# One buffer for a group's first-layer weights, 512-column matmuls for the leftover tile, and a shifted order, in a fused attention and expert kernel

## The chip, the cores and the metric

The kernel runs as one program on one core of a Trainium2 chip. The metric is device time in microseconds of one execution; lower is better. The engines are TensorE (PE), VectorE (DVE), ScalarE (ACT), GpSimd (POOL) and SyncE (SP), which issues the transfers. Each engine works through its own queue of instructions in program order and waits on semaphores for the others.

## The reference, cut to what matters

```python
# q, k, v: (2, 8, 576, 64); D = 512, E = 4, F = 1024, d_ff = 2048, N = 1152 tokens
x = windowed_causal_attention(q, k, v)            # window 128, linear bias by head
x = x.transpose(0, 2, 1, 3).reshape(1152, 512)
p = domain_probs / (domain_probs.sum(-1, keepdims=True) + 1e-09)
out = 0
for e in range(4):
    out += p[:, e:e + 1] * (np.maximum(x @ w1[e], 0.0) @ w2[e])
h = out @ w_in                                    # w_in, w_out are float64
return ((h * np.cos(h)) @ w_out).astype(np.float32)
```

## The kernel before

**Groups.** The two expert stages are cut into 12 groups of 512 hidden columns: groups 0 to 7 are the four experts' halves (Relu), groups 8 to 11 the last stage (h cos h). A group has a first layer (`pair`, twice, for its halves j = 0 and 1 of 256 columns) and a second layer (`layer2`, nine token tiles of 128 tokens). Every fp32 product is made of three passes over a high and a low part (`PASSES`: hi*hi, hi*lo, lo*hi).

**Tokens.** Tiles 1 to 8 (2 x 512 tokens) go through the first layer by seven block products instead of eight (`pair`, `product`), with 512 columns per matmul. Tile 0, the leftover of 128 tokens, goes through the first layer apart (`left(g)`, L732): its transposed tokens `x0` are the stationary operand and the weights `w1t` move, 256 columns at a time, 12 matmuls for each half j, both into one PSUM bank. Then ACT (L751) takes the Relu into the tile `lt` (groups 8 to 11: a cosine chain), and `turn_rows` (L768 to L771) transposes `lt` on PE, so that tile 0's hidden values are ready for the next group's second layer. `left(g + 1)` runs inside group g's second layer, in two steps called "La" and "Lb" (one half j each); "X" is `turn_rows`.

**Weights.** Raw weights come by DMA into two buffers (`rawp`), and a generator of jobs (`weights`, L207) splits them: ACT copies the high part (L201), POOL subtracts the low part (L178). "raw" is the half itself, "sums" its four block sums (POOL adds into `sm`, then the same split), "second" half of the second layer's weights. A first-layer half takes one of two `w1t` buffers. `order_of` sets the order of a group's jobs, `wq` that of their loads.

**Conversions.** The last stage's weights arrive as float64. `convert` turns them into float32 on the side, 32 pieces: ACT L288, DVE L290 and L294, DVE L298, ACT L300, DVE L303, then a store by SP. L300 may only start when L294 of the same piece is done, and sits in ACT's queue among everything else. They run during groups 0 to 5.

**Order.** `steps(g)` writes the order of PE's work by hand: for each entry of `order` it yields a step, how many stages of the cosine chains to advance, how many jobs to record (`njobs`) and how many conversion yields (`ncv`). `run` records, for each entry, first the PE work of the step, then the jobs, then the conversion yields, and last the rest of the step (for "Lb" that is L751, for a tile the accumulation on DVE, L886). So the place of an entry sets what stands ahead of its last part on ACT and DVE. In groups 1 to 6 the order before is

```python
order = (0, "La", 5, 6, 1, 7, "Lb", 2, 8, 3, "X", 4)
njobs = [1] * 8
ncv = {0: 2, "La": 3, 5: 3, 6: 3, 1: 3, 7: 3, "Lb": 2, 2: 2, 8: 2}
```

where an integer is a token tile of the second layer. In groups 8 to 10 "a5" is the first half of tile 5's matmuls, put ahead while ACT, DVE and POOL finish the cosine of the last products.

Of the kernel before, what the change touches and what calls it, by code (L numbers as in the profile page):

```python
# [11 lines left out]
F32R = mybir.dt.float32r  # L12
# [19 lines left out]
ND = DM // 128  # L32
# [10 lines left out]
PASSES = ((0, 0), (0, 1), (1, 0))  # L43
# [6 lines left out]


@with_exitstack
def tile_kernel(ctx, tc, qT, kT, v, probs, w1, w2, w_in, w_out, out):
    nc = tc.nc
    pool = lambda name, **kw: ctx.enter_context(tc.tile_pool(name=name, **kw))

# [2 lines left out]
    xp = pool("xp", bufs=1)  # L59
    zp = pool("zp", bufs=1)  # L60
    hp = pool("hp", bufs=1)
    w1p = pool("w1p", bufs=2)
    w2p = pool("w2p", bufs=W2S)
    accp = pool("accp", bufs=1)
    rawp = pool("rawp", bufs=RAWS)
# [108 lines left out]
    wi32 = dram.tile([DM, F2], F32, name="wi32")  # L174
    wo32 = dram.tile([F2, DM], F32, name="wo32")

    def sub(eng, out, a, b):
        eng.tensor_tensor(out=out, in0=a, in1=b, op=ALU.subtract)  # L178

    def rows(g):  # L180
        return (g // 2, slice((g % 2) * G, (g % 2 + 1) * G)) if g < NG1 else (None, slice((g - NG1) * G, (g - NG1 + 1) * G))

    raw_t, w_t = {}, {}

    def raw_load(kind, g, j):
        e, fs = rows(g)
        if kind == 1:
            t = rawp.tile([128, ND, 256], F32, name="raw", tag="raw")
            src = (wi32 if e is None else w1[e])[:, fs][:, j * 256 : (j + 1) * 256]
        else:  # L190
            t = rawp.tile([128, 2, DM], F32, name="raw", tag="raw")
            src = (wo32 if e is None else w2[e])[fs, :][j * 256 : (j + 1) * 256, :]
        nc.sync.dma_start(out=t, in_=src.rearrange("(m p) f -> p m f", p=128))
        raw_t[kind, g, j] = t

    def first_part(out, src):

        if mm is None:
            nc.gpsimd.tensor_copy(out, src)
        else:  # L200
            nc.scalar.activation(out=out, in_=src, func=AF.Copy)  # L201

    def weights():


        def two_parts(eng, hi, lo, src):
            n = src.shape[1] // 2  # L207
            for p in range(2):
                s = slice(p * n, (p + 1) * n)
                first_part(hi[:, s], src[:, s])  # L210
                sub(eng, lo[:, s], src[:, s], hi[:, s].bitcast(F32))
                yield

        raws = {}

        def first(g, j):
            raw = raws[j] = raw_t.pop((1, g, j))
            w = w_t[1, g, j] = w1p.tile([128, 2, 2, 1024], F32R, name="w1t", tag="w1t")
            yield from two_parts(nc.gpsimd, w[:, 0, 0], w[:, 1, 0], raw.rearrange("p m f -> p (m f)"))

        def first_sums(g, j):

            raw, w = raws[j], w_t[1, g, j]
            a11, a12 = raw[:, 0:2, 0:128], raw[:, 2:4, 0:128]
            a21, a22 = raw[:, 0:2, 128:256], raw[:, 2:4, 128:256]
            sm = ssp.tile([128, 4, 2, 128], F32, name="sm", tag="sm")
            nc.gpsimd.tensor_tensor(out=sm[:, 0], in0=a21, in1=a22, op=ALU.add)
            sub(nc.gpsimd, sm[:, 1], sm[:, 0], a11)
            yield
            sub(nc.gpsimd, sm[:, 2], a11, a21)  # L230
            sub(nc.gpsimd, sm[:, 3], a12, sm[:, 1])
            yield
            loads_ahead()
            yield from two_parts(nc.gpsimd, w[:, 0, 1], w[:, 1, 1], sm.rearrange("p s m f -> p (s m f)"))

        def second(g, j):
            raw = raw_t.pop((2, g, j))
            w = w_t[2, g, j] = w2p.tile([128, 2, 2, DM], F32R, name="w2t", tag="w2t")
            for f in range(2):
                first_part(w[:, 0, f], raw[:, f])  # L240
                sub(nc.gpsimd, w[:, 1, f], raw[:, f], w[:, 0, f].bitcast(F32))
                if f:
                    loads_ahead()
                yield

        for g in range(NG1 + NG2):
            for todo, j in order_of(g):
                yield from {"raw": first, "sums": first_sums, "second": second}[todo](g, j)

    def order_of(g):  # L250

        if g == 0 or g > NG1:
            return [("raw", 0), ("raw", 1), ("sums", 0), ("sums", 1), ("second", 0), ("second", 1)]
        return [("raw", 0), ("sums", 0), ("second", 0), ("raw", 1), ("sums", 1), ("second", 1)]

    wq = [
        (2 if todo == "second" else 1, g, j)
# [5 lines left out]
    def loads_ahead():  # L263

        if nload[0] < len(wq):
            raw_load(*wq[nload[0]])
            nload[0] += 1
# [64 lines left out]
    x0 = xp.tile([128, 2, ND, 128], F32R, name="x0")  # L332
# [355 lines left out]
    def cosine_rows(ps, out):  # L688

        for _ in cosine(ps, out):  # L690
            yield False

    def chain(c, ch):
        next(ch)
        chains.append((c, ch))
# [35 lines left out]
    def sums():  # L731
        return bank().tile([128, 512], F32, name="o_ps", tag="o_ps")  # L732
# [3 lines left out]
    def left(g):  # L736

        ps = sums()
        for j in range(2):
            for d in range(ND):  # L740
                for a, bb in PASSES:
                    nc.tensor.matmul(  # L742
                        ps[:, j * 256 : (j + 1) * 256], x0[:, bb, d, :],
                        w_t[1, g, j][:, a, 0, d * 256 : (d + 1) * 256],
                        start=(d == 0 and (a, bb) == PASSES[0]),
                        stop=(d == ND - 1 and (a, bb) == PASSES[-1]),
                    )
            yield
        r = rows_t[g] = lp.tile([128, 512], F32, name="lt", tag="lt")
        if g < NG1:  # L750
            nc.scalar.activation(out=r, in_=ps, func=AF.Relu)  # L751
        else:
            chain(0, cosine_rows(ps, r))
# [257 lines left out]
    def steps(g):  # L1011
# [6 lines left out]
        ps = [early.pop(j, None) or pair(g, j, early_kind) for j in range(2)]  # L1018
# [24 lines left out]
        if turn:  # L1043
            order = (0, 1, "f0", 5, "f1", 2, "f5", 6, "f2", 3, "f6", 4, "f3", 7, "f4", 8, "f7")
            njobs = [2, 2, 0, 2, 0, 2]
        elif moe:
            order = (0, "La", 5, 6, 1, 7, "Lb", 2, 8, 3, "X", 4)
            njobs = [1] * 8
            if g == 0:
                order = (0, "La", 5, 6, 1, 7, 2, "Lb", 8, 3, "X", 4)  # L1050
                njobs[0] = 2
                ncv = {5: 1, 6: 2, 1: 3, 7: 3, 2: 3, "Lb": 2, 8: 2}
        elif last:
            order, njobs = ("a5", "a6", "a7", "a8", "a1", 5, 6, 7, 8, 1, 2, 3, 4), []
        else:
            order = ("a5", "a6", "a7", "a8", "a1", "La", 5, 6, 7, "Lb", 8, 1, 2, "X", 3, 4)
            njobs = [0, 0, 0, 0, 0, 1, 1, 1, 1, 1, 1, 1, 1, 1, 1, 2]
        for k, o in enumerate(order):
            m = njobs.pop(0) if njobs else 0
            if isinstance(o, int):  # L1060
# [99 lines left out]
```

## Time and profile before

| | us |
|---|---|
| median of 3 runs | 646.12 (646.05 to 647.6) |
| the profiled execution | 647.3 |
| its span, first to last instruction | 645.5 |
| PE busy | 632.0 (98%) |
| DVE busy | 444.3 (69%) |
| POOL busy | 347.1 (54%) |
| ACT busy | 326.4 (51%) |
| granted TensorE clock, mean | 0.995 of full speed |

The profiled execution's own time is 1.8 us over its span and 1.2 us over the median. "Busy" counts the time in which an engine runs an instruction; matmuls overlap, so a line of the timeline that says 2.88 us for twelve matmuls can be followed by the next line 2.72 us after its start. What a stretch of matmuls takes is therefore read from start to start. In a timeline the bracket behind a row is the idle time of the engine ahead of it and what ended it.

### The profile page before, as it was taken

What the parts mean: (1) busy time and instruction counts of PE and PEld (TensorE: products, weight loads), DVE (VectorE), ACT (ScalarE), POOL (GpSimd) and SP (SyncE); (2) the same over time, 40 slices, a digit from 0 to 9 for tenths busy, and PEclk for the clock granted to TensorE, in tenths of its full rate; (3) what the DMA queues carried; (4) which work ended last, traced back from release to release, by engine and by line L of the source; (5) the groups of instructions that cost most, each with busy time, mean ns of one, the idle gap of its engine ahead of it and who ended that gap; (6) DMA issues with size and microseconds to landing.
All of it is one profiled execution on the core that took longest, in us unless ns stands there. A gap on an engine that the chain in (4) does not pass through costs nothing.

```text
span 645.5 us, 9428 instructions
## 1 busy us (share of the span) xinstructions
PE 632.0 (98%) x3456; PEld 520.6 (81%) x3456; DVE 444.3 (69%) x774; ACT 326.4 (51%) x690; POOL 347.1 (54%) x332
## 2 busy tenths in 40 slices
PE   8999699999999999999999999999999999999998
PEld 6777588888888888888888888888878888888876
DVE  6878658879879878779789543556873574664653
ACT  6998624444444353443443331455883583673650
POOL 1776439264275275185265390493469369379350
PEclk9999899999999999999999999999999999999999
DMA  9541214525517417427144120130001201201003
GB/s 255 140 147 52 98 32 147 156 89 179 164 56 223 146 45 255 125 80 231 65 155 140 32 80 20 34 98 1 26 7 63 69 2 66 65 1 65 17 2 130
DMA packets 39422, 60.66 MB, mean 94 GB/s; under 512 B 4688, under 2 KB 21840, under 8 KB 39376
## 3 DMA queue, kind: packets, MB, share of 16 engines
q1 hardware_dynamic: 38288, 59.67, 29.1%
q8 instruction: 27, 0.44, 0.3%
q10 hardware_dynamic: 1088, 0.39, 0.2%
q14 instruction: 19, 0.16, 0.1%
HBM read 49.30 MB, written 10.75 MB: 93 GB/s over the span
## 4 chain that ended last, share of the span: by engine, by line
PE 87%; ACT 5%; DVE 5%; issue 1%; DMA 1%; ACTq 0%; POOLq 0%; POOL 0%; DVEq 0%
PE o_ps L865 44%; PE o_ps L712 32%; PE o_ps L742 4%; PE x_ps L570 2%; PE s_ps L471 1%; PE t_ps L538 1%; ACT p L488 1%; DVE p L482 1%; DMA k<-kT 1%; ACT xs L342 1%; ACT u L665 1%; PE l_ps L768 1%; DVE tx L178 1%; ACT r L666 1%; PE f_ps L919 1%
## 5 line engine op out<-in xcount | busy, mean ns | idle before, releaser
L865 PE MATMUL o_ps<-w2t,hpair 128*128 128x512 f32 x1140 | 268.5, 392 | 0.6 <-POOL hpair L178 0.6
L865 PEld LDWEIGHTS o_ps<-w2t,hpair 128*128 128x128 f32 x1140 | 211.3, 188 | 44.0 <-POOL hpair L178 1.4
L712 PE MATMUL o_ps<-xs,w1t 128*128 128x512 f32 x720 | 170.3, 392 | 0.6 <-ACT rs L517 0.6
L712 PEld LDWEIGHTS o_ps<-xs,w1t 128*128 128x128 f32 x720 | 135.6, 189 | 29.2 <-ACT rs L517 0.7
L178 POOL TENSOR_TENSOR w1t<-raw,w1t 128x512 fp32r<-128x512 f32 x48 | 64.7, 1363 | 86.1 <-ACT w1t L201 85.8
L178 POOL TENSOR_TENSOR w2t<-raw,w2t 128x512 fp32r<-128x512 f32 x48 | 63.3, 1340 | 64.4 <-ACT w2t L201 64.3
L178 POOL TENSOR_TENSOR w1t<-sm,w1t 128x512 fp32r<-128x512 f32 x48 | 64.1, 1349 | 37.4 <-ACT w1t L201 34.3
L712 PE MATMUL o_ps<-xz,w1t 128*128 128x512 f32 x288 | 70.8, 392 | 0.9 <-DVE c L779 0.8
L178 POOL TENSOR_TENSOR hpair<-u,hpair 128x512 fp32r<-128x512 f32 x32 | 41.7, 1318 | 45.9 <-ACT hpair L685 45.9
L712 PEld LDWEIGHTS o_ps<-xz,w1t 128*128 128x128 f32 x288 | 53.6, 188 | 13.7 <-DVE c L779 2.5
L300 ACT ACTIVATE cr<-cr 128x512 f32<-128x512 f32 x32 | 21.8, 681 | 78.3 <-DVE cv L294 78.3
L886 DVE SCALAR_TENSOR_TENSOR accpair<-o_ps,pr,accpair 128x512 f32<-128x512 f32 x56 | 41.2, 745 | 28.0 <-PE o_ps L865 28.0
L702 DVE SCALAR_TENSOR_TENSOR hpair<-o_ps,hpair 128x512 fp32r<-128x512 f32 x47 | 32.4, 689 | 21.5 <-ACT hpair L701 21.5
L701 ACT ACTIVATE hpair<-o_ps 128x512 fp32r<-128x512 f32 x47 | 28.2, 599 | 36.0 <-DVE o_ps L779 36.0
L201 ACT ACTIVATE w1t<-sm 128x512 fp32r<-128x512 f32 x44 | 27.4, 625 | 30.4 <-POOL sm L178 30.4
L865 PE MATMUL o_ps<-w2t,h 128*128 128x512 f32 x144 | 36.5, 402 | 4.7 <-ACT xz L342 4.6
L742 PEld LDWEIGHTS o_ps<-w1t,x 128*128 128x128 f32 x288 | 37.5, 191 | 2.1 <-issue 0.3
L669 DVE SCALAR_TENSOR_TENSOR u<-r,u 128x512 f32<-128x512 f32 x36 | 30.0, 833 | 13.3 <-ACT r L666 13.2
L742 PE MATMUL o_ps<-w1t,x 128*128 128x256 f32 x288 | 38.4, 283 | 0.0
L701 ACT ACTIVATE hpair<-c 128x512 fp32r<-128x512 f32 x17 | 10.7, 632 | 51.8 <-DVE c L779 50.2
L865 PEld LDWEIGHTS o_ps<-w2t,h 128*128 128x128 f32 x144 | 27.6, 193 | 11.6 <-ACT xz L342 5.0
L892 DVE TENSOR_TENSOR accpair<-o_ps,accpair 128x512 f32<-128x512 f32 x23 | 15.7, 689 | 30.5 <-PE o_ps L865 30.5
(131 smaller groups left out, 891.6 us busy)
## 6 DMA issues: line engine op xcount, KB each, us to landing
raw<-w SPq DMA_DIRECT2D x32, 512.0 KB, 3.7
cr<-w_in SPq DMA_DIRECT2D x16, 512.0 KB, 4.5
cr<-w_out SPq DMA_DIRECT2D x16, 512.0 KB, 3.9
wi<-cv SPq DMA_DIRECT2D x16, 256.0 KB, 3.5
wo<-cv SPq DMA_DIRECT2D x16, 256.0 KB, 2.2
raw<-wi SPq DMA_DIRECT2D x8, 512.0 KB, 3.4
raw<-wo SPq DMA_DIRECT2D x8, 512.0 KB, 3.6
qt<-qT SPq DMA_DIRECT2D x8, 256.0 KB, 3.8
```

Of the source, the lines that this page charges most:

```text
L178: eng.tensor_tensor(out=out, in0=a, in1=b, op=ALU.subtract)
L201: nc.scalar.activation(out=out, in_=src, func=AF.Copy)
L300: nc.scalar.activation(out=fl(hw), in_=fl(hw), func=AF.Abs)
L570: nc.tensor.matmul(xt[64 * hh : 64 * hh + 64, 2 * g + m, :], v_t[b, j][:ln, 64 * h : 64 * h + 64], pT[:ln, 2 * m + hh, bi, :], start=(bi = ...
L669: nc.vector.scalar_tensor_tensor(out=u, in0=r, scalar=MAGIC, in1=u, op0=ALU.subtract, op1=ALU.subtract)
L701: nc.scalar.activation(out=hi, in_=src, func=AF.Relu)
L702: nc.vector.scalar_tensor_tensor(out=lo, in0=src, scalar=0.0, in1=hi.bitcast(F32), op0=ALU.max, op1=ALU.subtract)
L712: nc.tensor.matmul(ps, w(a, k, m), operand_of_x(bb, b)[:, m], start=(start and m == 0 and (a, bb) == PASSES[0]), stop=(stop and m == 1 and ...
L742: nc.tensor.matmul(ps[:, j * 256 : (j + 1) * 256], x0[:, bb, d, :], w_t[1, g, j][:, a, 0, d * 256 : (d + 1) * 256], start=(d == 0 and (a, ...
L865: nc.tensor.matmul(ps, hidden(a, f, t), w_t[2, g, f // 2][:, bb, f % 2, :], start=(f == 0 and (a, bb) == PASSES[0]), stop=(f == NFG - 1 an ...
L886: nc.vector.scalar_tensor_tensor(out=o, in0=ps, scalar=s, in1=o, op0=ALU.mult, op1=ALU.add)
L892: nc.vector.tensor_tensor(out=o, in0=ps, in1=o, op=ALU.add)
```

## The change

One tile `w1` holds both halves of a group's first-layer weights; each job writes its half of it. `left` moves 512 columns, 256 of each half, in one matmul, and its two steps are now the first and the last two blocks of the contraction instead of the two halves. Since both halves are then needed at "La", a group's jobs are recorded in another order (raw and sums of both halves ahead of "second"), "La" and "Lb" come later in the second layer, and groups 8 to 10 put one more tile ("a2") ahead.

```diff
--- before.py
+++ after.py
@@ -50,7 +50,7 @@
 
 
 @with_exitstack
-def tile_kernel(ctx, tc, qT, kT, v, probs, w1, w2, w_in, w_out, out):
+def tile_kernel(ctx, tc, qT, kT, v, probs, w_1, w_2, w_in, w_out, out):
     nc = tc.nc
     pool = lambda name, **kw: ctx.enter_context(tc.tile_pool(name=name, **kw))
 
@@ -59,7 +59,7 @@
     xp = pool("xp", bufs=1)
     zp = pool("zp", bufs=1)
     hp = pool("hp", bufs=1)
-    w1p = pool("w1p", bufs=2)
+    w1p = pool("w1p", bufs=1)
     w2p = pool("w2p", bufs=W2S)
     accp = pool("accp", bufs=1)
     rawp = pool("rawp", bufs=RAWS)
@@ -181,15 +181,16 @@
         return (g // 2, slice((g % 2) * G, (g % 2 + 1) * G)) if g < NG1 else (None, slice((g - NG1) * G, (g - NG1 + 1) * G))
 
     raw_t, w_t = {}, {}
+    w1 = w1p.tile([128, 2, 2, 2, 1024], F32R, name="w1t")
 
     def raw_load(kind, g, j):
         e, fs = rows(g)
         if kind == 1:
             t = rawp.tile([128, ND, 256], F32, name="raw", tag="raw")
-            src = (wi32 if e is None else w1[e])[:, fs][:, j * 256 : (j + 1) * 256]
+            src = (wi32 if e is None else w_1[e])[:, fs][:, j * 256 : (j + 1) * 256]
         else:
             t = rawp.tile([128, 2, DM], F32, name="raw", tag="raw")
-            src = (wo32 if e is None else w2[e])[fs, :][j * 256 : (j + 1) * 256, :]
+            src = (wo32 if e is None else w_2[e])[fs, :][j * 256 : (j + 1) * 256, :]
         nc.sync.dma_start(out=t, in_=src.rearrange("(m p) f -> p m f", p=128))
         raw_t[kind, g, j] = t
 
@@ -215,7 +216,7 @@
 
         def first(g, j):
             raw = raws[j] = raw_t.pop((1, g, j))
-            w = w_t[1, g, j] = w1p.tile([128, 2, 2, 1024], F32R, name="w1t", tag="w1t")
+            w = w_t[1, g, j] = w1[:, j]
             yield from two_parts(nc.gpsimd, w[:, 0, 0], w[:, 1, 0], raw.rearrange("p m f -> p (m f)"))
 
         def first_sums(g, j):
@@ -251,7 +252,7 @@
 
         if g == 0 or g > NG1:
             return [("raw", 0), ("raw", 1), ("sums", 0), ("sums", 1), ("second", 0), ("second", 1)]
-        return [("raw", 0), ("sums", 0), ("second", 0), ("raw", 1), ("sums", 1), ("second", 1)]
+        return [("raw", 0), ("sums", 0), ("raw", 1), ("sums", 1), ("second", 0), ("second", 1)]
 
     wq = [
         (2 if todo == "second" else 1, g, j)
@@ -736,16 +737,16 @@
     def left(g):
 
         ps = sums()
-        for j in range(2):
-            for d in range(ND):
-                for a, bb in PASSES:
-                    nc.tensor.matmul(
-                        ps[:, j * 256 : (j + 1) * 256], x0[:, bb, d, :],
-                        w_t[1, g, j][:, a, 0, d * 256 : (d + 1) * 256],
-                        start=(d == 0 and (a, bb) == PASSES[0]),
-                        stop=(d == ND - 1 and (a, bb) == PASSES[-1]),
-                    )
-            yield
+        for d in range(ND):
+            for a, bb in PASSES:
+                nc.tensor.matmul(
+                    ps.rearrange("p (j f) -> p j f", j=2), x0[:, bb, d, :],
+                    w1[:, :, a, 0, d * 256 : (d + 1) * 256],
+                    start=(d == 0 and (a, bb) == PASSES[0]),
+                    stop=(d == ND - 1 and (a, bb) == PASSES[-1]),
+                )
+            if d % 2:
+                yield
         r = rows_t[g] = lp.tile([128, 512], F32, name="lt", tag="lt")
         if g < NG1:
             nc.scalar.activation(out=r, in_=ps, func=AF.Relu)
@@ -1044,17 +1045,17 @@
             order = (0, 1, "f0", 5, "f1", 2, "f5", 6, "f2", 3, "f6", 4, "f3", 7, "f4", 8, "f7")
             njobs = [2, 2, 0, 2, 0, 2]
         elif moe:
-            order = (0, "La", 5, 6, 1, 7, "Lb", 2, 8, 3, "X", 4)
+            order = (0, 5, 6, 1, "La", 7, 2, "Lb", 8, 3, "X", 4)
             njobs = [1] * 8
             if g == 0:
-                order = (0, "La", 5, 6, 1, 7, 2, "Lb", 8, 3, "X", 4)
+                order = (0, 5, 6, 1, "La", 7, 2, "Lb", 8, 3, "X", 4)
                 njobs[0] = 2
                 ncv = {5: 1, 6: 2, 1: 3, 7: 3, 2: 3, "Lb": 2, 8: 2}
         elif last:
             order, njobs = ("a5", "a6", "a7", "a8", "a1", 5, 6, 7, 8, 1, 2, 3, 4), []
         else:
-            order = ("a5", "a6", "a7", "a8", "a1", "La", 5, 6, 7, "Lb", 8, 1, 2, "X", 3, 4)
-            njobs = [0, 0, 0, 0, 0, 1, 1, 1, 1, 1, 1, 1, 1, 1, 1, 2]
+            order = ("a5", "a6", "a7", "a8", "a1", "a2", 5, 6, 7, "La", 8, "Lb", 1, 2, 3, "X", 4)
+            njobs = [0, 0, 0, 0, 0, 0, 1, 1, 1, 1, 1, 1, 1, 1, 1, 1, 2]
         for k, o in enumerate(order):
             m = njobs.pop(0) if njobs else 0
             if isinstance(o, int):
```

The first place is PE's queue in the second layer of group 2 (L742 is `left`, L865 a token tile, L768 "X", L712 the next first layer). Before:

```order
L865 MATMUL o_ps<-w2t,h_138 128x512 x12
L742 MATMUL o_ps<-w1t,x_133 128x256 x12
L865 MATMUL o_ps<-w2t,hpair 128x512 x48
L742 MATMUL o_ps<-w1t,x_133 128x256 x12
L865 MATMUL o_ps<-w2t,hpair 128x512 x36
L768 MATMUL l_ps<-ident,lt 128x128 x4
L865 MATMUL o_ps<-w2t,hpair 128x512 x12
```

With the change (lines of other parts count one higher, so L866 is L865 and L769 is L768):

```order
L866 MATMUL o_ps<-w2t,h_139 128x512 x12
L866 MATMUL o_ps<-w2t,hpair 128x512 x36
L742 MATMUL o_ps<-w1t,x_134 128x512 x6
L866 MATMUL o_ps<-w2t,hpair 128x512 x24
L742 MATMUL o_ps<-w1t,x_134 128x512 x6
L866 MATMUL o_ps<-w2t,hpair 128x512 x24
L769 MATMUL l_ps<-ident,lt 128x128 x4
L866 MATMUL o_ps<-w2t,hpair 128x512 x12
```

The two blocks of leftover matmuls have 6 instructions of 512 columns each in place of 12 of 256; the first stands behind four tiles instead of one, the second behind six instead of five, and between the second and L768 there are now 24 matmuls where there were 36.

The second place is ACT's queue in the same group around `lt` (L751; L288 and L300 belong to conversions, L201 to weight jobs). Before:

```order
L300 ACTIVATE cr_2342<-cr_2342 128x512
L201 ACTIVATE w1t_2338<-sm_2389 128x512
L288 ACTIVATE cr_2368<-cr_2368 128x512
L751 ACTIVATE lt_2445<-o_ps_2305 128x512
L201 ACTIVATE w1t_2338<-sm_2389 128x512
L300 ACTIVATE cr_2368<-cr_2368 128x512
L288 ACTIVATE cr_2395<-cr_2395 128x512
L770 ACTIVATE h0_138<-l_ps_2501 128x512
```

With the change (L752 is L751, L301 is L300, L289 is L288, L202 is L201):

```order
L202 ACTIVATE w1t_132<-sm_2294 128x512
L301 ACTIVATE cr_2298<-cr_2298 128x512
L202 ACTIVATE w2t_2384<-raw_2220 128x512
L289 ACTIVATE cr_2324<-cr_2324 128x512
L202 ACTIVATE w2t_2384<-raw_2220 128x512
L301 ACTIVATE cr_2324<-cr_2324 128x512
L752 ACTIVATE lt_2408<-o_ps_2332 128x512
L289 ACTIVATE cr_2346<-cr_2346 128x512
L771 ACTIVATE h0_139<-l_ps_2446 128x512
```

The same conversion step that followed L751 before (L300 on `cr_2368`, now L301 on `cr_2324`) stands ahead of L752 with the change.

## Rows read from the trace of the kernel before

**Rows 1.** The page, parts 1 and 5: busy time by engine; the leftover's matmuls.

```profile
PE 632.0 (98%) x3456; PEld 520.6 (81%) x3456; DVE 444.3 (69%) x774; ACT 326.4 (51%) x690; POOL 347.1 (54%) x332
...
L742 PE MATMUL o_ps<-w1t,x 128*128 128x256 f32 x288 | 38.4, 283 | 0.0
```

**Rows 2.** Timeline of PE, group 2's second layer: start us, us, engine, line, operation, count.

```profile
186.98 2.88 PE L865 MATMUL o_ps<-w2t,h 128*128 128x512 f32 x12
189.70 1.59 PE L742 MATMUL o_ps<-w1t,x 128*128 128x256 f32 x12
191.13 11.07 PE L865 MATMUL o_ps<-w2t,hpair 128*128 128x512 f32 x48
202.04 1.59 PE L742 MATMUL o_ps<-w1t,x 128*128 128x256 f32 x12
203.47 8.35 PE L865 MATMUL o_ps<-w2t,hpair 128*128 128x512 f32 x36
211.66 0.60 PE L768 MATMUL l_ps<-ident,lt 128*128 128x128 f32 x4
```

**Rows 3.** Line L751 (the leftover's Relu): who waited for it, us and times.

```profile
  PEld l_ps L768: 0.3, 1
```

**Rows 4.** Timeline of ACT, group 2, around L751 (in brackets idle time before).

```profile
206.62 0.67 ACT L300 ACTIVATE cr<-cr 128x512 f32<-128x512 f32 x1 [2.21 <-DVE cv L294]
207.19 0.62 ACT L201 ACTIVATE w1t<-sm 128x512 fp32r<-128x512 f32 x1
207.71 0.65 ACT L288 ACTIVATE cr<-cr 128x512 int32<-128x512 uint32 x1
208.26 0.58 ACT L751 ACTIVATE lt<-o_ps 128x512 f32<-128x512 f32 x1
...
211.93 0.68 ACT L300 ACTIVATE cr<-cr 128x512 f32<-128x512 f32 x1 [2.56 <-DVE cv L294]
```

**Rows 5.** Timeline of ACT: the conversion step before L751's new place, groups 1, 3, 4, 5; L751 in 6.

```profile
162.85 0.68 ACT L300 ACTIVATE cr<-cr 128x512 f32<-128x512 f32 x1 [2.49 <-DVE cv L294]
...
259.27 0.70 ACT L300 ACTIVATE cr<-cr 128x512 f32<-128x512 f32 x1 [2.55 <-DVE cv L294]
...
302.26 0.68 ACT L300 ACTIVATE cr<-cr 128x512 f32<-128x512 f32 x1 [2.48 <-DVE cv L294]
...
350.50 0.68 ACT L300 ACTIVATE cr<-cr 128x512 f32<-128x512 f32 x1 [2.48 <-DVE cv L294]
...
391.35 0.60 ACT L751 ACTIVATE lt<-o_ps 128x512 f32<-128x512 f32 x1 [6.74 <-PE o_ps L742]
```

**Rows 6.** Timeline of PE: where the second layer of groups 1, 3, 4 and 5 begins.

```profile
140.05 2.88 PE L865 MATMUL o_ps<-w2t,h 128*128 128x512 f32 x12
...
233.88 2.88 PE L865 MATMUL o_ps<-w2t,h 128*128 128x512 f32 x12
...
280.82 2.88 PE L865 MATMUL o_ps<-w2t,h 128*128 128x512 f32 x12
...
327.73 2.88 PE L865 MATMUL o_ps<-w2t,h 128*128 128x512 f32 x12
```

**Rows 7.** Timelines of DVE and POOL, groups 2 and 3: conversions beside POOL's subtractions.

```profile
204.85 0.68 DVE L303 SCALAR_TENSOR_TENSOR cv<-cr,cv 128x512 f32<-128x512 f32 x1
...
207.95 1.78 DVE L303 SCALAR_TENSOR_TENSOR cv<-cr,cv 128x512 f32<-128x512 f32 x1
...
207.88 1.29 POOL L178 TENSOR_TENSOR w1t<-sm,w1t 128x512 fp32r<-128x512 f32 x1 [3.02 <-ACT w1t L201]
...
244.30 0.64 DVE L290 TENSOR_SCALAR cv<-cr 128x512 int32<-128x512 int32 x1 [2.04 <-DMA wo<-cv]
...
241.94 2.71 POOL L178 TENSOR_TENSOR w1t<-raw,w1t 128x512 fp32r<-128x512 f32 x2 [2.33 <-ACT w1t L201]
```

**Rows 8.** Timelines of PE and POOL, group 8: its second layer's start; half 1's low parts.

```profile
477.06 5.17 PE L865 MATMUL o_ps<-w2t,hpair 128*128 128x512 f32 x21
...
486.01 2.55 POOL L178 TENSOR_TENSOR w1t<-raw,w1t 128x512 fp32r<-128x512 f32 x2
```

## The prediction

> **What bounds the kernel now.** I read the page first: PE is busy for 632.0 of the 645.5 us of the span, the next engine, DVE, for 444.3 [rows 1]. So PE's own time counts one for one, and every other engine counts only where it makes PE wait. The timeline of PE came second: in a second layer each row starts where the row before it hands over, with no gap in brackets [rows 2]. The third view was who waits for the leftover's Relu, L751, since it is the one result of ACT whose user, the transposes "X", comes closer to it with the change: over the whole run PE waited 0.3 us for it, once [rows 3]. The last views were the timelines of ACT and DVE around L751, which show what stands next to it there [rows 4, 5].
>
> The sum below is made against the profiled execution (647.3 us, span 645.5); a change in the span is carried over to the median of the runs shown, 646.12, which lies 1.2 us lower. A difference of 0.3%, 1.94 us, is about what a measurement of this kernel can tell from no change.
>
> **Term 1: the leftover's matmuls.** Removed: 24 matmuls of 256 columns per group, 288 in all [rows 1]. Added: 12 of 512 per group. From start to start twelve of 256 take 191.13 - 189.70 = 1.43 us and the second dozen 203.47 - 202.04 = 1.43 us, so a group pays 2.86 us. Twelve of 512 take 189.70 - 186.98 = 2.72 us [rows 2]. A group saves 0.14 us, twelve groups 1.68 us, if one matmul that moves two pieces of 256 columns costs as much as one that moves 512 in a row. No row shows a move in two pieces. The lower bound of its price is 2.72 us a dozen, since as many columns pass; the upper bound is that a piece costs what a matmul of 256 costs, 2.86 us, and nothing is saved. I take 2.72: the row of the same width is the nearest.
>
> By these rows a matmul costs 2 x 1.43 - 2.72 = 0.14 us per dozen pairs, or 12 ns, beside its columns. The Trainium skill, "TensorE: Matmul & The Clock Gate", section "Wait — 56ns, not 53.3ns?", gives a fixed cost of about 2.5 ns for a back-to-back matmul; by that the 144 matmuls that fall away would save an estimated 0.36 us, and the change would come out 1.32 us slower than by the rows, at an estimated 649.8. These rows disagree with it, and the rows decide.
>
> **Term 2: the Relu that the transposes wait for.** In groups 1 to 6 "X" used to stand three tiles behind "Lb" and now stands two behind. With the rates of rows 2 (a tile 10.91 / 4 = 2.73 us, the first 2.72, half a leftover 1.36) PE now reaches X at 2.72 + 3 x 2.73 + 1.36 + 2 x 2.73 + 1.36 + 2 x 2.73 = 24.55 us after the second layer began; before it was 211.66 - 186.98 = 24.68 [rows 2]. So X is due as early as ever. L751, however, moves one entry later in ACT's queue, behind whatever the tile ahead of "Lb" records: a weight copy and two conversion yields. ACT is not busy there, but it is held: each L300 waits for L294 of its piece on DVE, 2.21 and 2.56 us in group 2 [rows 4], since DVE is still at the conversions before. What stands ahead of L751 depends on the phase of the conversions, which shifts from group to group. With the steps of ACT's queue from rows 4 (L300 0.57, L201 0.52, L288 0.55, L751 itself 0.58):
>
> - Group 2: before, L751 started at 208.26 and was done 2.8 us ahead of X. Now it follows the L300 of 211.93: done at 211.93 + 0.57 + 0.58 = 213.08, that is 26.10 after 186.98 [rows 2, 4]. X waits 1.55 us.
> - Group 3: it follows the L300 of 259.27, done at 260.42, 26.54 after 233.88 [rows 5, 6]. X waits 1.99 us.
> - Group 1: the L300 of 162.85 stood ahead of it before too; now L201 and L288 come between. Done at 162.85 + 0.57 + 0.52 + 0.55 + 0.58 = 165.07, 25.02 after 140.05 [rows 5, 6]. X waits 0.47 us.
> - Group 4: the same from 302.26, done 23.66 after 280.82 [rows 5, 6]: 0.89 us to spare.
> - Group 5: from 350.50 with only L201 between, done 24.44 after 327.73 [rows 5, 6]: 0.11 us to spare.
> - Group 6 has no conversions: L751 waits for PE itself, 6.74 us before [rows 5]. In group 0 neither X nor L751 moves against the other. Nothing there.
>
> PE takes its queue in order, so these waits, 1.55 + 1.99 + 0.47 = 4.01 us, are paid in full; the next first layer starts later by as much, and no later slack exists on PE to give it back.
>
> How firm is DVE's pace? Its list up to those L294 is the same as before, as many conversions and as many accumulations, and POOL has as many subtractions to make; the weight jobs only change places. A conversion on DVE takes 0.68 us alone and 1.78 beside a subtraction of POOL [rows 7], so each meeting more or fewer moves the chain by 1.1 us, and I put one meeting per group on either side as the bound. Group 3 has one thing more: DVE stood idle for 2.04 us until a store of converted weights had landed [rows 7], because SP held that store behind a raw load that waited for a buffer. The change takes that load out of that place. But during the pause POOL made two subtractions, 2.71 us [rows 7], which will now meet DVE at work. I take the two as equal, and keep the full 2.04 us as the lower end: then group 3 waits for nothing.
>
> **The rest, at nothing.** The half-1 weights must be ready at "La" now. In groups 1 to 6 that is four tiles, 10.9 us, after their jobs are recorded. In groups 8 to 10 it is closest: in group 8 POOL's low parts of half 1 end at 486.01 + 2.55 = 488.56, while "La" comes after 6 half tiles and 3 more, 9 x 1.36 = 12.24 us after 477.06, at 489.30 [rows 8]; covered by 0.74 us, and only from its third matmul on. If that cover went, it would cost its lateness, three times at most. "a2" takes the place of "La" as cover for the cosine, 1.36 for 1.43 us. "second" is ready later but is needed a first layer later. The raw load that held SP's store moves to behind "La", where it waits for POOL's sums of half 1; if it held a store there, DVE would pause again, 2.04 us [rows 7], which is inside the upper bound below. One buffer instead of two adds no wait, since each write waits only for the readers of its own piece.
>
> **Sum.** 4.01 - 1.68 = +2.33 us: 648.5 us as a median, and 649.6 for an execution like the profiled one.
>
> **The rivals.**
> - *The Relu is not late.* The conversions run ahead of their old pace in groups 1 to 3 by 0.47, 1.55 and 1.99 us, because SP's pause is gone and subtractions fall beside accumulations. Then only term 1 is left: 646.12 - 1.68 = 644.4, not slower. For it: the pause of 2.04 us, and that one missed meeting (1.1 us) frees group 1. Against it: group 2 had no such pause and is late by more than one meeting. Chance 0.13; a little over half of it passes 0.3%.
> - *It is late in part.* Group 3 is healed by the lost pause, the others stay: 0.47 + 1.55 - 1.68 = +0.34, 646.5. Or each meets POOL a little less. Chance 0.33, all within 0.3%.
> - *Two pieces cost two moves.* Term 1 is nothing: +4.01, 650.1. For it: no row shows a move in two pieces. Against it: the same columns and half the instructions. Chance 0.08, slower.
>
> **How the numbers follow.** The forecast has what is left, 0.46, all slower by over 0.3%; its own range is 647.6 (a meeting less) to 650.5 (two more). Slower: 0.46 + 0.08 for the third rival = 0.54. Faster by over 0.3%: 0.08, the part of the first rival that gains 0.3 us on top. Within: 0.33 + the other 0.05 of the first rival = 0.38. For 8 in 10 the range must reach into the first rival but need not hold its lower part, and ends at the forecast's upper end: 644.9 to 650.5.
>
> **What would show it.** Right: PE's waits name L768 or its weight load as waiting for ACT's lt, three times, about 1.5, 2.0 and 0.5 us, in groups 2, 3 and 1; in the timeline L751 follows an L300; L742 has 144 matmuls of 512 columns, twelve of them in 2.72 us from start to start. Wrong in term 2: no wait at the transposes, and L300 ahead of L751 less than 24 us after the second layer begins. Wrong in term 1: a dozen at 2.8 us or more. Wrong in the rest: a wait of PE at L742 for POOL, in groups 8 to 10 above all.

## The result, and the profile after

The changed kernel takes 651.85 us (median of 6 runs, 650.44 to 653.36), the kernel before 646.83 us (6 runs, 646.05 to 647.92): ratio 1.0077, 95% interval 1.0056 to 1.0098, or 5.0 us more. The profiled execution took 652.47 us, its span 650.7. The forecast was 648.5 with a range up to 650.5: the sign was right, the size less than half.

The page of the changed kernel, first the busy times, then the leftover's matmuls (answering to [rows 1]):

```profile
PE 631.3 (97%) x3312; PEld 512.5 (79%) x3312; DVE 447.0 (69%) x774; ACT 327.3 (50%) x690; POOL 347.0 (53%) x332
...
L742 PE MATMUL o_ps<-w1t,x 128*128 128x512 f32 x144 | 36.8, 391 | 0.0
```

PE is busy for 0.7 us less, in a span 5.2 us longer. So PE waits more, and the view of what PE waited for says on what (line waited for: us in total, times, longest):

```profile
PE l_ps L769 <- ACT lt L752: 5.3, 4, 2.1
PE o_ps L866 <- ACT xz L343: 4.6, 1, 4.6
PE o_ps L948 <- DVE dens L946: 1.2, 1, 1.2
```

The second and third stood there before as well, with the same numbers. The first is new: the transposes "X" wait for the leftover's Relu, four times. The timeline of PE in group 2's second layer shows one of them (answering to [rows 2]):

```profile
188.88 2.88 PE L866 MATMUL o_ps<-w2t,h 128*128 128x512 f32 x12
191.59 8.32 PE L866 MATMUL o_ps<-w2t,hpair 128*128 128x512 f32 x36
199.75 1.52 PE L742 MATMUL o_ps<-w1t,x 128*128 128x512 f32 x6
201.12 5.60 PE L866 MATMUL o_ps<-w2t,hpair 128*128 128x512 f32 x24
206.56 1.52 PE L742 MATMUL o_ps<-w1t,x 128*128 128x512 f32 x6
207.91 5.60 PE L866 MATMUL o_ps<-w2t,hpair 128*128 128x512 f32 x24
215.61 0.66 PE L769 MATMUL l_ps<-ident,lt 128*128 128x128 f32 x4 [2.09 <-ACT lt L752]
```

Six matmuls in two pieces take 1.36 us from start to start, twelve 2.72, as forecast. X comes 26.73 us after the second layer began, not 24.55. The timeline of ACT there shows why (answering to [rows 4]):

```profile
209.28 0.67 ACT L301 ACTIVATE cr<-cr 128x512 f32<-128x512 f32 x1 [2.49 <-DVE cv L295]
209.85 0.62 ACT L202 ACTIVATE w2t<-raw 128x512 fp32r<-128x512 f32 x1
210.37 0.66 ACT L289 ACTIVATE cr<-cr 128x512 int32<-128x512 uint32 x1
210.93 0.61 ACT L202 ACTIVATE w2t<-raw 128x512 fp32r<-128x512 f32 x1
214.40 0.69 ACT L301 ACTIVATE cr<-cr 128x512 f32<-128x512 f32 x1 [2.86 <-DVE cv L295]
214.97 0.58 ACT L752 ACTIVATE lt<-o_ps 128x512 f32<-128x512 f32 x1
```

L752's sums are ready shortly after 207.9, where the second half's matmuls end; ACT stands idle for 2.86 us with L752 behind an L301 that waits for DVE's L295. This is the mechanism of term 2. Its size comes from DVE and POOL at the same time (DVE first, then POOL):

```profile
209.74 0.69 DVE L299 CUSTOM_DVE_ANT_0 cv<-cr,cv 128x1024 uint16<-128x1024 uint16 x1 [0.49 <-DVE cv L295]
...
211.81 0.87 DVE L291 TENSOR_SCALAR cv<-cr 128x512 int32<-128x512 int32 x1
212.71 1.66 DVE L295 SCALAR_TENSOR_TENSOR cv<-cr,cv 128x512 int32<-128x512 int32 x1
...
210.54 3.28 POOL L178 TENSOR_TENSOR w2t<-raw,w2t 128x512 fp32r<-128x512 f32 x2 [2.30 <-ACT w2t L202]
```

L295, the very step that ACT waits for, takes 1.66 us instead of 0.69 beside POOL's subtraction for the second layer's weights, which the new order of the jobs puts here. The 0.49 us in the first row's bracket is DVE waiting for its own result.

Where the time goes by group, as periods from one second layer's start to the next (read from PE's rows as in [rows 6]), in us, with the idle time at X in parentheses:

| group | before | after | X at the end (see below) |
|---|---|---|---|
| 0 | 45.55 | 45.77 | 45.77 |
| 1 | 46.93 | 48.00 (1.08) | 46.74 |
| 2 | 46.90 | 49.03 (2.09) | 46.70 |
| 3 | 46.94 | 48.52 (1.59) | 46.74 |
| 4 | 46.91 | 46.73 | 46.70 |
| 5 | 46.93 | 47.48 (0.54) | 46.74 |
| 6 | 46.90 | 46.71 | 46.70 |

The stage ahead of group 0 varies from profile to profile, also between kernels that are the same up to there: group 0's second layer began between 93.44 and 95.11 us in the eleven profiles read here (94.50 before, 95.11 after). The periods are free of that, so the readings below go by periods, and by medians where a kernel as a whole is judged.

### The profile page after: what moved, and what is told of

It is laid out like the page before. It is cut to its first block, busy times and chain, and to the rows that moved or that the text cites. A ratio compares the mean times of both kernels' runs of the same rounds, so it can differ in the third digit from the quotient of the medians.

```text
span 650.7 us, 9171 instructions
## 1 busy us (share of the span) xinstructions
PE 631.3 (97%) x3312; PEld 512.5 (79%) x3312; DVE 447.0 (69%) x774; ACT 327.3 (50%) x690; POOL 347.0 (53%) x332
## 4 chain that ended last, share of the span: by engine, by line
PE 69%; DVE 18%; ACT 7%; issue 4%; DMA 1%; POOLq 0%; DVEq 0%; ACTq 0%; POOL 0%
PE o_ps L866 30%; PE o_ps L713 29%; DVE cv L295 3%; DVE cv L291 3%; PE o_ps L742 3%; DVE cv L304 2%; DVE cv L299 2%; PE s_ps L472 2%; PE x_ps L571 2%; DVE hpair L703 1%; PE t_ps L539 1%; ACT hpair L702 1%; DVE c L780 1%; ACT p L489 1%; DVE p L483 1%
## 5 line engine op out<-in xcount | busy, mean ns | idle before, releaser
L866 PE MATMUL o_ps<-w2t,hpair 128*128 128x512 f32 x1140 | 269.5, 391 | 0.6 <-POOL hpair L178 0.6
L866 PEld LDWEIGHTS o_ps<-w2t,hpair 128*128 128x128 f32 x1140 | 212.4, 188 | 45.7 <-POOL hpair L178 1.4
L178 POOL TENSOR_TENSOR w2t<-raw,w2t 128x512 fp32r<-128x512 f32 x48 | 63.0, 1331 | 90.0 <-ACT w2t L202 88.0
L178 POOL TENSOR_TENSOR w1t<-raw,w1t 128x512 fp32r<-128x512 f32 x48 | 65.1, 1374 | 69.7 <-ACT w1t L202 68.7
L178 POOL TENSOR_TENSOR w1t<-sm,w1t 128x512 fp32r<-128x512 f32 x48 | 62.8, 1326 | 31.9 <-ACT w1t L202 31.6
L178 POOL TENSOR_TENSOR hpair<-u,hpair 128x512 fp32r<-128x512 f32 x32 | 41.7, 1315 | 45.9 <-ACT hpair L686 45.9
L301 ACT ACTIVATE cr<-cr 128x512 f32<-128x512 f32 x32 | 21.7, 678 | 78.0 <-DVE cv L295 78.0
L703 DVE SCALAR_TENSOR_TENSOR hpair<-o_ps,hpair 128x512 fp32r<-128x512 f32 x47 | 32.4, 688 | 21.5 <-ACT hpair L702 21.5
L202 ACT ACTIVATE w1t<-sm 128x512 fp32r<-128x512 f32 x44 | 27.6, 626 | 33.1 <-POOL sm L178 33.0
L866 PE MATMUL o_ps<-w2t,h 128*128 128x512 f32 x144 | 36.5, 402 | 4.7 <-ACT xz L343 4.6
L304 DVE SCALAR_TENSOR_TENSOR cv<-cr,cv 128x512 f32<-128x512 f32 x32 | 36.5, 1141 | 3.0 <-ACT cr L301 1.6
L489 ACT ACTIVATE p<-p,nmax 128x256 f32<-128x256 f32 (+2 forms) x72 | 33.5, 472 | 7.5 <-DVE nmax L483 7.4
L742 PE MATMUL o_ps<-w1t,x 128*128 128x512 f32 x144 | 36.8, 391 | 0.0
L866 PEld LDWEIGHTS o_ps<-w2t,h 128*128 128x128 f32 x144 | 27.6, 193 | 11.6 <-ACT xz L343 5.0
```

Source lines behind the costliest of these rows:

```text
L301: nc.scalar.activation(out=fl(hw), in_=fl(hw), func=AF.Abs)
L304: nc.vector.scalar_tensor_tensor(out=fl(o), in0=fl(hw), scalar=TINY, in1=fl(a), op0=ALU.is_ge, op1=ALU.mult,)
L489: nc.scalar.activation(out=p[:, k, :wid], in_=p[:, k, :wid], func=AF.Exp, scale=-1.0, bias=nmax[:, k : k + 1], accum_out=den[:, k, 0:1],)
L703: nc.vector.scalar_tensor_tensor(out=lo, in0=src, scalar=0.0, in1=hi.bitcast(F32), op0=ALU.max, op1=ALU.subtract)
L742: nc.tensor.matmul(ps.rearrange("p (j f) -> p j f", j=2), x0[:, bb, d, :], w1[:, :, a, 0, d * 256 : (d + 1) * 256], start=(d == 0 and (a, ...
L866: nc.tensor.matmul(ps, hidden(a, f, t), w_t[2, g, f // 2][:, bb, f % 2, :], start=(f == 0 and (a, bb) == PASSES[0]), stop=(f == NFG - 1 an ...
```

## The experiments

The theory: the loss is the wait at X, since L752 stands behind a conversion that DVE holds; the matmuls' saving is real. The main rivals: the loss lies elsewhere in the change, or the wait has another cause (DVE late as a whole, the new order of the jobs). All run on the changed kernel unless said.

**X at the end.** Groups 1 to 6.

```diff
-            order = (0, 5, 6, 1, "La", 7, 2, "Lb", 8, 3, "X", 4)
+            order = (0, 5, 6, 1, "La", 7, 2, "Lb", 8, 3, 4, "X")
```

> In groups 1 to 6 the transposes "X" go behind tile 4 instead of ahead of it; all else as in the change. If the Relu that reaches ACT's queue late is what costs the time: X is due a tile (2.73 us) later, the changed kernel's largest lateness is 2.2 us, so the four waits at L769 (5.3 us in all) vanish, the time falls by 5.3 us to about 646.5 us, and against the kernel before only the 1.7 us of the leftover's matmuls and some 0.4 us lost in group 0 are left: 645.5. Rival, the loss lies in the job order (ACT, DVE and POOL behind in all of the second layer): X moves and something else waits, time within 1 us of 651.9.

Measured: 645.86 us, ratio to before 0.9975 (0.9964 to 0.9985). No matmul of PE waits for L752 any more, and groups 1 to 6 take 46.70 to 46.74 us each (table above). One more tile, 2.72 us, ahead of X covers the Relu, and the whole loss is gone. This version is faster than the changed kernel, and by 0.25% than the kernel before.

**Conversions behind the Relu.** The conversion yields that "Lb" records, ahead of L752, are recorded by tile 8 instead.

```diff
-        ncv = {0: 2, "La": 3, 5: 3, 6: 3, 1: 3, 7: 3, "Lb": 2, 2: 2, 8: 2}
+        ncv = {0: 2, "La": 3, 5: 3, 6: 3, 1: 3, 7: 3, "Lb": 0, 2: 2, 8: 4}
```

> In groups 1 to 6 the two conversion yields of the entry "Lb" are recorded one entry later (ncv 0 for "Lb", 4 for tile 8); PE's order as in the change. Conversions between tile 2 and the Relu stay. If conversions ahead of the Relu in ACT's queue hold it: the L301 ahead of L752 goes in groups 2 and 3 (waits 2.1 and 1.6 us become 0), in group 1 only an L289 of 0.55 us goes (1.1 becomes 0.5), in group 5 nothing changes (0.5). Waits 5.3 us become about 1.1, time about 647.7. Rival, the order of PE alone makes X early against everything: waits stay near 5 us, time near 651.9.

Measured: 646.61 us, ratio 0.9990 (0.9979 to 1.0001). The waits of groups 2 and 3 are gone; 0.54 and 0.55 us are left in groups 1 and 5. In group 1 the L301 still stands ahead, only the L289 behind it has left, and the wait is shorter by that step (1.08 to 0.54 us):

```profile
162.61 0.68 ACT L301 ACTIVATE cr<-cr 128x512 f32<-128x512 f32 x1 [1.95 <-DVE cv L295]
163.19 0.62 ACT L202 ACTIVATE w2t<-raw 128x512 fp32r<-128x512 f32 x1
163.71 0.58 ACT L752 ACTIVATE lt<-o_ps 128x512 f32<-128x512 f32 x1
```

**Lb one place earlier.** X stays where it is.

```diff
-            order = (0, 5, 6, 1, "La", 7, 2, "Lb", 8, 3, "X", 4)
+            order = (0, 5, 6, 1, "La", 7, "Lb", 2, 8, 3, "X", 4)
```

> In groups 1 to 6 the leftover's second half stands one tile earlier (behind tile 7, ahead of tile 2), and the Relu with it; X stays. If the loss is the Relu's place in ACT's queue, behind the conversion that DVE holds: no wait at X in any group, about 645.9 us, as with X at the end. If the loss is that DVE's conversions as a whole run late, wherever the Relu stands: waits at X remain and the time stays over 649 us.

Measured: 645.86 us, ratio 0.9981 (0.9969 to 0.9992). In group 2 the same L301 still comes as late (25.52 us after the second layer's start, here and in the changed kernel), but L752 now stands ahead of it:

```profile
207.68 0.66 ACT L289 ACTIVATE cr<-cr 128x512 int32<-128x512 uint32 x1
208.24 0.58 ACT L752 ACTIVATE lt<-o_ps 128x512 f32<-128x512 f32 x1
208.72 0.62 ACT L202 ACTIVATE w2t<-raw 128x512 fp32r<-128x512 f32 x1
211.71 0.68 ACT L301 ACTIVATE cr<-cr 128x512 f32<-128x512 f32 x1 [2.37 <-DVE cv L295]
```

So a late DVE alone costs nothing in group 2; the Relu's place in ACT's queue decides. Groups 1 and 5 take 46.96 us, 0.2 more than the others, and that is a rest of the same wait: there an L301 still stands ahead of L752 (162.70 in group 1), L752 ends at 163.27 + 0.58 = 163.85, and the weight load of X starts right behind it, 24.67 us after the second layer began and not 24.49 as in group 2:

```profile
163.90 0.42 PEld L769 LDWEIGHTS l_ps<-ident,lt 128*128 128x128 f32 x4 [0.45 <-ACT lt L752]
```

The expected absence of any wait was missed by these 0.2 us in two groups.

**Lb one place later, alone.** The kernel before with this one edit; 256 columns, jobs and "La" as before.

```diff
-            order = (0, "La", 5, 6, 1, 7, "Lb", 2, 8, 3, "X", 4)
+            order = (0, "La", 5, 6, 1, 7, 2, "Lb", 8, 3, "X", 4)
```

> The kernel before with one thing of the change: the leftover's second half one tile later (behind tile 2), X in its place; the first half behind tile 0, the 256 columns and the order of the jobs as before. If the Relu's place behind the held conversion is the whole cause: waits at X as forecast, about 0.3, 1.4 and 1.9 us in groups 1, 2 and 3, none in 4 and 5, each with 0.2 us on top, 4.2 us together: about 651.4 us on this chip. If the wait needs the first half's move or the new order of the jobs as well: under 649 us.

Measured: 650.89 us, ratio 1.0066 (1.0051 to 1.0082). PE idles at X for 0.21, 1.31 and 1.74 us in groups 1, 2 and 3 and not at all in 4 and 5, each 0.1 to 0.2 us less than expected. By periods the three groups lose 0.41, 1.55 and 1.92 us, 3.9 together. This single move makes most of the loss. In group 2 the L300 starts 212.39 - 187.44 = 24.95 us after the second layer, to the hundredth where it stood before [rows 2, 4]:

```profile
212.39 0.67 ACT L300 ACTIVATE cr<-cr 128x512 f32<-128x512 f32 x1 [3.04 <-DVE cv L294]
212.96 0.58 ACT L751 ACTIVATE lt<-o_ps 128x512 f32<-128x512 f32 x1
```

**The old order of the jobs.**

```diff
-        return [("raw", 0), ("sums", 0), ("raw", 1), ("sums", 1), ("second", 0), ("second", 1)]
+        return [("raw", 0), ("sums", 0), ("second", 0), ("raw", 1), ("sums", 1), ("second", 1)]
```

> The weight jobs of groups 1 to 8 in the order of before (second-layer half 0 between the two first-layer halves); PE's order as in the change. The forecast's waits (0.5, 1.55, 2.0 and 0 us in groups 1, 2, 3 and 5, 4.0 in all) took DVE's pace of before, which had this job order. If the job order is what made the waits 5.3 us (POOL meets DVE's conversions more often): 4.0 us here, time about 650.5, and the pause of DVE for a store in group 3 is back. Rival, the pace has nothing to do with the job order: 5.3 us again, about 651.9.

Measured: 654.18 us, ratio 1.0098 (1.0082 to 1.0113), against both expectations. Two things not thought of come on top. In group 0 half 1's weights are late for "La" now:

```profile
107.49 1.19 PE L742 MATMUL o_ps<-w1t,x 128*128 128x512 f32 x4 [2.06 <-POOL w1t L178]
```

so with "La" at its new place the old order is too slow there. And in group 3 the wait is followed by a fall of the clock (last section). The run still tells one thing apart: with the old jobs PE idles at X for 0.39, 2.13 and 1.97 us in groups 1, 2 and 3, and not in 4 and 5. The forecast was 0.47, 1.55, 1.99, 0 and 0. So the longer waits of groups 1 and 5 (1.08 and 0.54) belong to the new order of the jobs, group 2's does not. The pause of DVE for a store in group 3 is back only in part: 0.58 and 0.28 us, where it was 2.04 [rows 7].

**Second jobs behind the Relu.** Two of the four jobs for the second layer's weights move from tile 2 and "Lb" to tiles 8 and 3 (groups 1 to 6).

```diff
-            njobs = [1] * 8
+            njobs = [1, 1, 1, 1, 1, 1, 0, 0, 1, 1]
```

> The changed kernel; the two jobs that make the first copies and low parts of the second layer's weights are recorded at tiles 8 and 3, behind the Relu, in place of tile 2 and Lb. If these jobs made the waits longer than forecast (their copy stands ahead of the Relu in ACT's queue, 0.52 us in groups 1 and 5, and their subtraction on POOL meets DVE's conversion, about 1.0 us): no wait at X in groups 1, 3 and 5, about 1.1 us in group 2, and about 647.0 us. If it is only where DVE's accumulations fall among the conversions: group 2 stays at 2.1 and group 3 at 1.6 us, groups 1 and 5 lose the copy's 0.5 us, about 651 us.

Measured: 645.79 us, ratio 0.9986 (0.9976 to 0.9996). One wait is left, 0.68 us in group 2. No job stood between L301 and L752 there, so its 1.41 us less come from DVE's pace alone: without POOL's subtraction beside them L291 and L295 take 0.42 and 0.69 us, not 0.87 and 1.66:

```profile
207.22 0.69 DVE L299 CUSTOM_DVE_ANT_0 cv<-cr,cv 128x1024 uint16<-128x1024 uint16 x1 [0.50 <-DVE cv L295]
...
209.29 0.42 DVE L291 TENSOR_SCALAR cv<-cr 128x512 int32<-128x512 int32 x1
209.75 0.69 DVE L295 SCALAR_TENSOR_TENSOR cv<-cr,cv 128x512 int32<-128x512 int32 x1
...
212.22 2.90 POOL L178 TENSOR_TENSOR w2t<-raw,w2t 128x512 fp32r<-128x512 f32 x2 [6.51 <-ACT w2t L202]
```

**256 columns in the changed kernel.** Each matmul of `left` is split into one per half, in the same places; the two halves add up by turns in one PSUM bank, so the leftover's sums come out different in this kernel.

```diff
-                    ps.rearrange("p (j f) -> p j f", j=2), x0[:, bb, d, :],
-                    w1[:, :, a, 0, d * 256 : (d + 1) * 256],
+                for j in range(2):
...
+                    ps[:, j * 256 : (j + 1) * 256], x0[:, bb, d, :],
+                    w1[:, j, a, 0, d * 256 : (d + 1) * 256],
```

> The leftover's matmuls move 256 columns of one half each again (24 a group), in the places, the buffer and the job order of the change. By the start-to-start times (2.86 us against 2.72 a group) twelve groups lose 1.7 us; each X is due 0.1 us later, so four waits give 0.4 us back: about 653.1. Rival, pairing two pieces saves nothing: 651.9 or below.

Measured: 651.99 us, ratio 1.0066 (1.0054 to 1.0079): no difference to the changed kernel in the median, where 653.1 was expected. By periods, groups 4 and 6, which don't wait, are longer by 0.20 us (46.94 and 46.91); groups 1, 3 and 5, which do, are not (48.04, 48.52, 47.48), since X waits there for ACT however early PE comes. Where a wait follows, time saved ahead of it is no gain. Group 2 is even shorter by 0.59 us (48.44): 7.7 us into its second layer an L299 of DVE and a subtraction of POOL start within 0.02 us of each other in both kernels, and here L299 takes 0.67 us and POOL 1.30, there 1.27 and 0.74. So the L301 ahead of the Relu starts 24.93 us after the second layer and not 25.52: which of the two engines is held moved this wait by half a us. The question needs a base without waits:

**256 columns with X at the end.** The loops of `left` as before, half by half, in the first kernel above.

```diff
+        for j in range(2):
             for d in range(ND):
                 for a, bb in PASSES:
...
-                    w1[:, :, a, 0, d * 256 : (d + 1) * 256],
+                    w1[:, j, a, 0, d * 256 : (d + 1) * 256],
```

> The kernel with X at the end, with the leftover's 24 matmuls of 256 columns, half by half as before, in place of 12 of 512. No wait at X hides the difference here. By the prediction's rows (0.14 us per group, 12 groups): 1.68 us more than with X at the end, 647.5 us. By the group periods of the run with 256 columns against those of the change (46.94 against 46.73 us in group 4, 46.91 against 46.71 in group 6, 0.20 per group): 2.4 us more, 648.3 us. If a matmul in two pieces had saved nothing: 645.9 us.

Measured: 647.0 us, ratio to before 1.0008 (0.9997 to 1.0018), against 0.9975 with 512 columns: 0.33% or 2.1 us, uncertain by about 1. The periods are sharper: 46.94 and 46.90 in turn, against 46.74 and 46.70. Group 4, 256 columns (L743 is `left`):

```profile
291.80 1.59 PE L743 MATMUL o_ps<-w1t,x 128*128 128x256 f32 x12
293.23 5.63 PE L866 MATMUL o_ps<-w2t,hpair 128*128 128x512 f32 x24
298.70 1.59 PE L743 MATMUL o_ps<-w1t,x 128*128 128x256 f32 x12
300.13 8.35 PE L866 MATMUL o_ps<-w2t,hpair 128*128 128x512 f32 x36
308.32 0.60 PE L769 MATMUL l_ps<-ident,lt 128*128 128x128 f32 x4
```

and 512 columns:

```profile
291.62 1.52 PE L742 MATMUL o_ps<-w1t,x 128*128 128x512 f32 x6
292.98 5.60 PE L866 MATMUL o_ps<-w2t,hpair 128*128 128x512 f32 x24
298.42 1.52 PE L742 MATMUL o_ps<-w1t,x 128*128 128x512 f32 x6
299.78 8.33 PE L866 MATMUL o_ps<-w2t,hpair 128*128 128x512 f32 x36
307.94 0.60 PE L769 MATMUL l_ps<-ident,lt 128*128 128x128 f32 x4
```

A block of twelve costs 1.43 against 1.36 us, and the block behind it 5.47 against 5.44 and 8.19 against 8.16: 2 x 0.07 + 2 x 0.03 = 0.20 us a group. From group 0's second layer to the end the two profiles differ by 1.8 us for eleven leftovers, so not every group gains the 0.20.

**Group 0 as before.** X at the end, but group 0 has its old order again, and 256 columns half by half (`if g == 1` in `left`).

```diff
-                order = (0, 5, 6, 1, "La", 7, 2, "Lb", 8, 3, "X", 4)
+                order = (0, "La", 5, 6, 1, 7, 2, "Lb", 8, 3, "X", 4)
```

> The kernel with X at the end; in group 0 alone the leftover is computed as before: 24 matmuls of 256 columns, its first half directly behind tile 0. If group 0 loses 0.4 us because tile 5 now follows tile 0 at once and finds the low parts of its hidden values not ready: the 36 matmuls of tiles 5, 6 and 1 take 8.16 us from start to start as before, not 8.59, and group 0's period is 45.55 us, as before the change, not 45.77: 0.2 us less in all, which only the periods can show, and about 645.7 us. If the 0.4 us have another cause: the 36 matmuls still take 8.59 us, and the period is 45.97 us.

Measured: 646.02 us, ratio 0.9985 (0.9976 to 0.9994). The reason holds: behind "La" the 60 matmuls of five tiles take 110.57 - 96.94 = 13.63 us, as before the change, where directly behind tile 0 the 36 of three tiles took 105.05 - 96.47 = 8.58 in the changed kernel (60 at 13.63 make 36 at 8.18). There DVE made a low part (L703) from 97.78 to 98.47, and a matmul of tile 5 starts at 98.53, 0.39 us behind the one before it, where 0.23 is usual. But the period is 46.30 us, longer than either expectation, since X waits here too (lines of other parts count eleven higher: L877 is L866, L780 is L769, L763 is L752):

```profile
96.94 13.79 PE L877 MATMUL o_ps<-w2t,hpair 128*128 128x512 f32 x60
110.57 1.60 PE L744 MATMUL o_ps<-w1t,x 128*128 128x256 f32 x12
...
118.16 0.66 PE L780 MATMUL l_ps<-ident,lt 128*128 128x128 f32 x4 [0.53 <-ACT lt L763]
...
114.70 0.43 DVE L291 TENSOR_SCALAR cv<-cr 128x512 int32<-128x512 int32 x1 [3.53 <-DMA wi<-cv]
```

The last row says why group 0, which had this order before without a wait, waits now: DVE stands idle for 3.53 us until a store of converted weights has landed, and the L301 ahead of the Relu comes late by it. The store's values were ready at 105.58, but SP issued it only at 109.40, behind a raw load at 108.93 that had waited for POOL's sums. It is the held store that the prediction names as a risk, here in another kernel.

## Why the prediction was wrong in size

**What bounds: right.** PE's time counts one for one; every loss is found as a wait of PE or as a stretch of its matmuls.

**Term 1: right, and slightly too small.** Forecast 0.14 us a group, measured 0.20: the forecast priced the blocks of 256 and left out the 0.03 us that each costs the block behind it. Two pieces of 256 move as fast as 512 in a row, so the third rival is out. Twelve groups at 0.20 are 2.4 us, and the two profiles with X at the end differ by 1.8 us for eleven. The Trainium skill's "TensorE: Matmul & The Clock Gate", section "Wait — 56ns, not 53.3ns?", would have given an estimated 0.36 us in all; the trace doesn't agree with it.

**Term 2: the mechanism right, the size not; this is the step that failed.** Forecast 4.01 us. Measured against the periods with X at the end, groups 1, 2, 3 and 5 lose 1.26, 2.33, 1.78 and 0.74 us: 6.11. The 2.10 us between have three parts:
- +0.48 by the run with the old jobs: 2.13 for 1.55 in group 2, and -0.08 and -0.02 in groups 1 and 3 (the match in group 3 is in part luck, since DVE's pause there is 0.58 and 0.28 us and not the 2.04 of the rows). The prediction said that DVE's list up to L294 stays "the same as before, as many conversions and as many accumulations". As many, yes, but since "La" no longer stands behind tile 0, PE hands over its tiles at other times, and no accumulation fills the gap that DVE leaves between L295 and L299: the bracket of 0.49 us above (0.50 with the old jobs). In the kernel before, the accumulation L886 stood in that gap (rows below).
- +0.81 by the new order of the jobs (0.69, -0.04, -0.38 and 0.54 in groups 1, 2, 3 and 5). The prediction kept POOL's meetings with DVE as they were, with one meeting (1.1 us) per group as a bound. In group 1 the sixteen conversion steps from L299 at 147.02 to L295 at 162.57 are busy for 14.54 us by DVE's timeline; the same sixteen took 13.84 with the old jobs (149.14 to 164.01). That is the 0.69 us: the same list, met more often. In group 3 the forecast wait was indeed shorter (1.59 for 1.99): DVE's pause for the store is gone and meetings took its place, as weighed. Group 5 had "0.11 us to spare", well inside its bound, and was still counted as nothing.
- +0.81 over all four waits: a wait costs 0.18 to 0.24 us more than its bracket says. The transposes behind a wait take 0.41 us to the next start, not 0.36, and the bracket counts from a modelled end which in an unbroken row lies about 0.16 us behind the next start (1.52 for 1.36).

The gap of the first part, filled, in the kernel before (timeline of DVE, group 2):

```profile
205.90 0.69 DVE L294 SCALAR_TENSOR_TENSOR cv<-cr,cv 128x512 int32<-128x512 int32 x1
206.50 0.75 DVE L886 SCALAR_TENSOR_TENSOR accpair<-o_ps,pr,accpair 128x512 f32<-128x512 f32 x1
207.17 0.68 DVE L298 CUSTOM_DVE_ANT_0 cv<-cr,cv 128x1024 uint16<-128x1024 uint16 x1
```

With the old jobs and "La" back behind tile 0 (Lb later, alone) L300 starts at 24.95 us as before; with the old jobs and "La" late, L301 starts at 25.57. These two kernels also differ in the columns per matmul, but the run with 256 columns in the changed kernel has the same gap of 0.49, so the gap comes with La's move; that the 0.6 us come through the gap is read from the rows alone.

A meeting is seen in the rows above: the conversion L295, which reads two operands, takes 0.69 us alone and 1.66 beside POOL's L178. The Trainium skill's "SBUF — State Buffer", section "Who interferes with whom", states that a DVE instruction with two SBUF inputs contends with a GpSimd instruction that reads SBUF, since both use a shared pair of ports under an exclusive lock. The trace agrees with it.

**The rest at nothing: right but for group 0.** No row waits for half 1's weights, in groups 8 to 10 neither. "Nothing there" for group 0 looked at X and L751 alone: tile 5 now directly follows tile 0 and its low parts of the hidden values come late, 0.4 us, inside a row of 36 matmuls with no bracket. The pause of DVE for a held store, weighed there as a risk, is in no group of the changed kernel; it is in group 0 of the last experiment, with 3.53 us.

**The sum.** From group 0's second layer to the end the changed kernel takes 650.7 - 95.11 = 555.59 us, before it was 645.5 - 94.50 = 551.00: +4.59. Waits 6.11, group 0 0.41, less 11 leftovers at 0.20 (the twelfth lies ahead), 2.2, make 4.3; most of the 0.3 left is group 7, which did not get shorter (55.47 for 55.50). The other 0.6 us of the profiled pair lie ahead of group 0.

**The range** ended at two meetings more in all, put at 650.5, though 648.5 + 2 x 1.1 is 650.7 (and a meeting less 647.4, not 647.6). The bound that the text itself gives, one meeting per group, was not carried into it: for groups 1, 2, 3 and 5 it makes 3 x 1.1 + 1.1 - 0.11 = 4.3 us, or 652.8, above the 651.85 measured. The range also left out that the accumulations move too, counted group 5's cover of 0.11 us as safe, and took the brackets for the whole price of a wait.

## What to carry to other kernels

A result that another engine waits for belongs in its queue ahead of anything that is itself held, and its distance to the user should be counted from what stands in front of it, not from when its operands are ready; here one entry in a hand-written order cost 4 to 6 us and gave nothing. When a reorder leaves an engine's list of work the same, look again at when each piece arrives: a gap that used to be filled and one more meeting of two engines moved the chain here by 0.5 to 1 us each, without a longer list. A saving ahead of a wait is not a saving; take the wait away first, then measure it.

## What the runs showed of the hardware

A wait of PE may cost more than itself. In the profile with the old jobs the 1.97 us at X in group 3 were followed by a fall of the granted clock (timeline of PE, then by stretch: us, PE busy, PEld, DVE, ACT, POOL, PEclk, DMA share, GB/s):

```profile
265.99 0.66 PE L769 MATMUL l_ps<-ident,lt 128*128 128x128 f32 x4 [1.97 <-ACT lt L752]
266.40 4.58 PE L866 MATMUL o_ps<-w2t,hpair 128*128 128x512 f32 x12
270.80 6.99 PE L713 MATMUL o_ps<-xs,w1t 128*128 128x512 f32 x30
```

```profile
266.00:268.60 2.60, 2.60 (x11) 2.22 (x12) 2.46 (x6) 1.11 (x2) 0.00 (x0) 0.77 0.44 147
268.60:271.00 2.40, 2.40 (x7) 1.86 (x6) 1.20 (x2) 0.00 (x0) 0.00 (x0) 0.53 0.58 207
271.00:275.00 4.00, 4.00 (x19) 3.29 (x19) 1.44 (x2) 1.64 (x3) 1.42 (x2) 1.00 0.01 2
```

At 0.53 of 2.4 GHz, nearly all of the stretch at 1.2 GHz, the last tile's twelve matmuls took 270.80 - 266.40 = 4.40 us instead of 2.85: 1.55 us on top of the wait. That the wait causes the fall is not shown: the 2.13 us in group 2 of the same profile and the 2.09 us in the changed kernel's had none behind them (1.00 from 217.00 to 226.00, and from 215.60 to 219.00). Whether it happens in other executions of the changed kernel, and makes part of their spread of 3 us, no trace here shows. Their mean granted clock is 0.992 at 653.36 and 652.91 us and 0.994 to 0.997 in the other four; but three of 27 executions of the kernel before, which has no such wait, have 0.992 too (648.60 to 649.05 us).

A matmul whose moving operand comes in two pieces of 256 columns, one from each half of the buffer, costs the same as one of 512 in a row: 1.36 us for six.
